# Last addition of a decoded weight piece moved from GpSimd to VectorE, and both y^T evictions put on ScalarE

## The chip, the core and the metric

The kernel runs on one core of a Trainium2 chip. The metric is device time in microseconds (us), the median of several runs. A core has five engines that work through queues of their own and wait for each other by semaphores: TensorE (PE in the profile; its weight loads are PEld), VectorE (DVE), ScalarE (ACT), GpSimd (POOL) and SyncE (SP), which here issues all DMAs. Each queue is worked in order: an instruction that waits holds up all that stand behind it on its engine.

## What is computed

The weights w_in, w_out, w1, w2, w3 and w_out2 come as float64, all else as float32. Three blocks follow each other:

```python
p_packed = sm_attn(p, k, v)             # 8 batches x 8 heads, 32 packed rows, 576 keys, head size 64
out = sm_attn(q, p_packed, p_packed)    # 576 queries against the 32 packed rows
x = out.transpose(0, 2, 1, 3).reshape(4608, 512)
h = x @ w_in                            # 512 -> 1024
solu = h * softmax(h)
y = layernorm(solu) * g_ln @ w_out      # 1024 -> 512
h2 = maximum(maximum(y @ w1, y @ w2), y @ w3)   # 512 -> 768
result = h2 @ w_out2                    # 768 -> 512
```

## The kernel before

Matrix products are done on float32 values split into a high and a low part, three products for one, so that every product of a pair of 128-row blocks stands three times in a row on TensorE.

The program has three stages. In **stage one** (to about 505 us of the span) 36 tiles of 128 tokens pass through attention (class `Packed`, two batches ahead), `tok_hidden` (the product with `w_in`, line 511, and the softmax and layer norm arithmetic around it, lines 517 to 536), `y_transpose` (four transposes into PSUM, line 577, then `lh` on ScalarE, line 583, and `ll` on VectorE, line 584) and `y_product` (line 602). `y_product` makes y^T for 512 tokens at a time in two halves of two PSUM banks, y0 and y1, with eight steps a half; each step does three products into y0 and then three into y1. When the eighth step of a half is done, both banks are copied to SBUF tiles `yt` (two buffers) by the helper `ev`, and stored to `ydram` (line 610). There are 9 blocks of 512 tokens, so 18 halves and 36 copies. The key `yt` of the table `CFG` names the engine of each: 'sv' means ScalarE for y0 (line 242) and VectorE for y1 (line 244).

Beside this, stage one **decodes weights**. A float64 weight is two 32-bit words, which are turned into float32 with arithmetic on the words. A piece of 128x256 weights (`decode_piece`) takes a load into `raw` (two buffers, line 222), one ScalarE step into `dt` (line 116), four VectorE steps (lines 121, 124, 127 and 129) and one last addition of two SBUF operands, `wt` <- `raw`, line 132. `dt` and `wt` have one buffer each. There are 56 such pieces. The first 8 belong to `w_out` (`decode_w_out2`): their `wt` is rounded into `woh` on ScalarE (line 211) and the rest into `wol` on GpSimd (line 212), and `wt` is free when both have read it. The other 48 (`decode_w2`, for w1, w2, w3 and w_out2) are stored to DRAM by a DMA (line 234), and `wt` is free when that store has landed. The key `d2` names the engine of line 132 for these pieces: 'g' is GpSimd. The larger decodes of `w_in` and of the first half of `w_out` have keys of their own (`d0`, `d1`), which stay.

The **transition** (about 505 to 560 us) ends the last block of y, reads the decoded w1 to w3 and y^T back, and splits them into parts (`split_w`, lines 650 to 657; `splits_y`, lines 724 and 725); the Newton steps that make the layer norm scales (lines 545 to 568, on 128x36 values) also start here. **Stage two** (to the end) runs 54 cells (`cell`, products on line 748, with VectorE additions `u`, `v`, `r`, `cur`, `kept` at lines 767 to 796) and the last product (line 995).

The order of instructions on each engine is not the order of the source: a list scheduler lays out all queues from its own idea of what each instruction takes. So a change of one instruction's engine also shifts others.

Of the kernel before, what the change touches and what calls it, by code (L numbers as in the profile page):

```python
# [18 lines left out]
def f32(ap):  # L19
# [7 lines left out]
    e1T='s',  # L27
    ppT='sv',
    pTz='s',
    yt='sv',  # L30
    look=3,
    s0=['LFLTFLDH', 'FFTFHD', 'FTH', 'LDFFFTDFDDHFDL'],
    s1='DFNTAHTDTyATyDyTAFy',
# [11 lines left out]
    yt_tag='e1T',  # L45
    d0='gggg',
    d1='g',
    d2='g',
    ln4='vsvs',
)  # L50

# [1043 lines left out]
```

## Time and profile before

| | us |
|---|---|
| runs before | 1118.19, 1113.46, 1114.99 |
| median | 1114.99 |
| profiled execution, device time | 1115.81 |
| its span (first to last instruction) | 1114.0 |
| PE busy | 1045.9 (94%) |
| PEld busy | 875.5 (79%) |
| VectorE busy | 734.1 (66%) |
| ScalarE busy | 480.3 (43%) |
| GpSimd busy | 274.0 (25%) |
| mean granted TensorE clock | 0.983 of full |

The span is what the trace covers; 1.8 us of the device time lie around it. Matmuls overlap, so PE that is busy throughout need not be at its peak. The shares are means over stages that differ. The rows on which the prediction rests stand in a section of their own, below.

### The profile page before, as it was taken

How to read it: one execution, taken by the hardware profiler on the slowest of the kernel's cores; microseconds unless marked ns; L12 is line 12 of the kernel's file. 1: busy time of each engine (PE TensorE's matmuls, PEld its weight loads, DVE VectorE, ACT ScalarE, POOL GpSimd, SP SyncE). 2: the span in 40 equal slices, each digit the busy share in tenths (PEclk: the TensorE clock that was granted, in tenths of full speed). 3: DMA queues.
4: the chain of work that ended last, by engine and by line, in shares of the span. 5: the costliest groups of instructions: out<-in, count | busy, mean ns of one | idle time of the engine just before them, and what ended most of it. 6: DMA issues, size and time to landing. Idle time of an engine off the chain costs nothing.

```text
span 1114.0 us, 18016 instructions
## 1 busy us (share of the span) xinstructions
PE 1045.9 (94%) x6548; PEld 875.5 (79%) x6548; DVE 734.1 (66%) x1454; ACT 480.3 (43%) x935; POOL 274.0 (25%) x283
## 2 busy tenths in 40 slices
PE   4688999999999999999789999999999999999998
PEld 2456667676767667787678999989989999998996
DVE  5778797869787886756687735735664583571560
ACT  4586766666666667456333311331131131132112
POOL 3541311111102110104576410320041041132002
PEclk9798999999999999999899999999999999999999
DMA  9752546554555623400664534534454463343421
GB/s 259 171 131 69 162 113 177 136 145 134 144 156 134 165 85 99 133 20 28 238 222 145 170 118 126 164 114 134 140 161 133 122 185 110 114 124 109 128 76 57
DMA packets 132264, 149.04 MB, mean 134 GB/s; under 512 B 51536, under 2 KB 85328, under 8 KB 132176
## 3 DMA queue, kind: packets, MB, share of 16 engines
q1 hardware_dynamic: 132176, 147.89, 45.8%
q8 instruction: 52, 0.85, 0.3%
q14 instruction: 36, 0.29, 0.1%
HBM read 113.25 MB, written 34.60 MB: 133 GB/s over the span
## 4 chain that ended last, share of the span: by engine, by line
PE 51%; DVE 6%; issue 3%; ACT 2%; POOL 2%; DMA 1%; SPq 0%; DVEq 0%; POOLq 0%; ACTq 0%
PE m L748 30%; PE o L995 13%; PE y L602 4%; PE h L511 2%; POOL s L651 1%; PE tp L577 1%; DVE s L657 1%; DMA wt<-wdram 1%; ACT u L536 0%; DVE v L787 0%; POOL al L651 0%; DVE nm L517 0%; DVE u L521 0%; DVE r L770 0%; DVE ll L584 0%
## 5 line engine op out<-in xcount | busy, mean ns | idle before, releaser
L602 PE MATMUL y<-lh,woh 128*128 128x512 f32 x288 | 118.7, 416 | 1.0 <-ACT lh L583 0.8
L783 DVE TENSOR_TENSOR u<-m,q 128x384 f32<-128x384 f32 x54 | 29.9, 553 | 133.6 <-ACT ob L1004 75.8
L602 PE MATMUL y<-ll,woh 128*128 128x512 f32 x288 | 115.9, 402 | 0.1
L602 PE MATMUL y<-lh,wol 128*128 128x512 f32 x288 | 114.7, 398 | 0.0
L779 ACT COPY q<-m 128x384 f32<-128x384 f32 x54 | 25.9, 480 | 168.4 <-PE m L748 168.2
L810 POOL TENSOR_TENSOR hl<-cur,hh 128x384 fp32r<-128x384 f32 x36 | 37.4, 1040 | 244.2 <-ACT hh L809 244.1
L132 POOL TENSOR_TENSOR wt<-raw 128x256 f32<-128x256 f32 x56 | 35.2, 628 | 244.5 <-DVE raw L129 144.3
L995 PE MATMUL o<-w2h,hh 128*128 128x512 f32 x216 | 85.3, 395 | 0.0
L995 PE MATMUL o<-w2h,hl 128*128 128x512 f32 x216 | 85.3, 395 | 0.0
L995 PE MATMUL o<-w2l,hh 128*128 128x512 f32 x216 | 85.3, 395 | 0.0
L748 PE MATMUL m<-b22h,s 128*128 128x384 f32 x216 | 65.7, 345 | 2.3 <-DVE r L770 2.0
L602 PEld LDWEIGHTS y<-lh,woh 128*128 128x128 f32 x288 | 54.0, 189 | 15.4 <-issue 2.0
L748 PE MATMUL m<-t2h,s 128*128 128x384 f32 x216 | 64.2, 337 | 0.0
L602 PEld LDWEIGHTS y<-ll,woh 128*128 128x128 f32 x288 | 55.0, 191 | 11.7 <-DVE ll L584 0.5
L602 PEld LDWEIGHTS y<-lh,wol 128*128 128x128 f32 x288 | 54.5, 189 | 12.2
L748 PE MATMUL m<-t1h,s 128*128 128x384 f32 x216 | 63.7, 335 | 0.1
L748 PE MATMUL m<-t3h,s 128*128 128x384 f32 x216 | 63.5, 334 | 0.0
L809 ACT CAST hh<-cur 128x384 fp32r<-128x384 f32 x36 | 18.5, 514 | 89.7 <-DVE cur L796 49.1
L583 ACT ACTIVATE lh<-tp,g_sb 128x512 fp32r<-128x512 f32 x72 | 47.3, 692 | 22.7 <-PE tp L577 22.4
L810 POOL TENSOR_TENSOR hl<-kept,hh 128x384 fp32r<-128x384 f32 x36 | 38.9, 1082 | 72.3 <-ACT hh L809 72.3
L771 DVE TENSOR_TENSOR kept<-r,kept 128x384 f32<-128x384 f32 x72 | 55.2, 767 | 2.0
L584 DVE SCALAR_TENSOR_TENSOR ll<-tp,g_sb,lh 128x512 fp32r<-128x512 f32 x72 | 51.8, 742 | 6.3 <-ACT lh L583 6.2
(189 smaller groups left out, 2872.1 us busy)
## 6 DMA issues: line engine op xcount, KB each, us to landing
s<-sdram SPq DMA_DIRECT2D x180, 256.0 KB, 2.9
kt<-in_k_dram SPq DMA_DIRECT2D x16, 576.0 KB, 5.2
vt<-in_v_dram SPq DMA_DIRECT2D x16, 576.0 KB, 4.8
ydram<-yt SPq DMA_DIRECT2D x36, 256.0 KB, 2.5
raw<-in_moe_w_dram SPq DMA_DIRECT2D x36, 256.0 KB, 2.8
b<-ydram SPq DMA_DIRECT2D x24, 384.0 KB, 3.4
sdram<-s SPq DMA_DIRECT2D x36, 256.0 KB, 2.1
out_dram<-ob SPq DMA_DIRECT2D x36, 256.0 KB, 2.1
```

What stands on the lines that cost most here:

```text
L132: add.tensor_tensor(out=dst, in0=f32(hi), in1=f32(lo), op=ALU.add)
L511: nc.tensor.matmul(h[:, n, :], lhsT=x, rhs=m[:, g, n * 512:(n + 1) * 512], start=(i == 0), stop=(i == len(ops) - 1),)
L583: last[nc.scalar] = nc.scalar.activation(lh, tp, AF.Copy, scale=gc)
L584: last[nc.vector] = nc.vector.scalar_tensor_tensor(out=ll, in0=tp, scalar=gc, in1=f32(lh), op0=ALU.mult, op1=ALU.subtract)
L602: nc.tensor.matmul(ys[half][m], lhsT=w[:, kc, ms], rhs=x, start=(kc == 0 and i == 0), stop=(kc == KFF - 1 and i == 2),)
L748: nc.tensor.matmul(out, lhsT=w, rhs=y, start=start and i == 0, stop=i == len(ops) - 1, skip_group_check=not start,)
L771: add(out=cur[m, n], in0=r, in1=cur[m, n], op=ALU.max)
L779: nc.scalar.copy(q, ba)
L783: add(out=u, in0=bb, in1=q, op=ALU.add)
L809: nc.scalar.copy(hh, t)
L810: nc.gpsimd.tensor_tensor(out=hl, in0=t, in1=f32(hh), op=ALU.subtract)
L995: nc.tensor.matmul(ops[i], lhsT=x[:, ts], rhs=w, start=(c == 0 and n == 0), stop=(c == KF2 - 1 and n == 2),)
```

## The change

Two keys of the table change. The last addition of the 56 decoded pieces of 128x256 goes from GpSimd to VectorE, and the copy of y1 goes from VectorE to ScalarE, so that ScalarE makes both copies of a half. No tile, buffer or DMA is added or taken away.

```diff
-    yt='sv',
+    yt='s',
...
-    d2='g',
+    d2='v',
```

How the queues move is shown at three places. In all rows a name before the arrow is the tile written and those behind it are read; the bracket names the engines or DMA queues that the instruction waits for.

The VectorE queue at a `w_out` piece, in stage one at about 110 us. Before:

```order
L535 TENSOR_TENSOR nmu<-nmu,powers 128x1 [waits DVE_49]
L121 TENSOR_SCALAR dt<-dt 128x256 [waits Activation_49]
L124 SCALAR_TENSOR_TENSOR raw<-raw,dt 128x256 [waits DMAHW6_49,DVE_49,Pool_49]
L127 TENSOR_SCALAR dt<-raw 128x256 [waits DVE_49]
L129 SCALAR_TENSOR_TENSOR raw<-raw,dt 128x256 [waits DVE_49]
L517 TENSOR_REDUCE nm<-h 128x1 [waits PE_49]
L584 SCALAR_TENSOR_TENSOR ll<-tp,g_sb,lh 128x512 [waits Activation_49] x2
```

The same place after:

```order
L535 TENSOR_TENSOR nmu<-nmu,powers 128x1 [waits DVE_49]
L121 TENSOR_SCALAR dt<-dt 128x256 [waits Activation_49]
L124 SCALAR_TENSOR_TENSOR raw<-raw,dt 128x256 [waits DMAHW6_49,DVE_49]
L127 TENSOR_SCALAR dt<-raw 128x256 [waits DVE_49]
L129 SCALAR_TENSOR_TENSOR raw<-raw,dt 128x256 [waits DVE_49]
L132 TENSOR_TENSOR wt<-raw 128x256 [waits DVE_49,Pool_49]
L517 TENSOR_REDUCE nm<-h 128x1 [waits PE_49]
L584 SCALAR_TENSOR_TENSOR ll<-tp,g_sb,lh 128x512 [waits Activation_49] x2
```

The addition of line 132 stands behind line 129 and waits there for GpSimd, which reads the piece before it out of `wt`; for the 48 later pieces it waits for the store DMA instead.

The ScalarE queue in the transition (s, ah and ch are parts of w1 to w3; the numbered y are the banks of the last two halves), as a difference:

```order
 L242 COPY yt<-y_6009 128x512
 L650 CAST s_6198<-s_6176 128x256
+L242 COPY yt<-y_6010 128x512
+L650 CAST s_6216<-s_6208 128x256
 L650 CAST ah_2_6407<-wt_6302 128x512
-L650 CAST s_6216<-s_6208 128x256
 L650 CAST s_6228<-s_6220 128x256
 L650 CAST s_6234<-s_6206 128x256
 L650 CAST s_6248<-s_6232 128x256
 L650 CAST ch_2_6465<-wt_6304 128x256
-L242 COPY yt<-y 128x512
+L242 COPY yt<-y 128x512 x2
```

The copies of y1 have joined those of y0, one a place or two behind it, and one rounding of a weight part has moved ahead of another.

The VectorE queue at the first cell of stage two (z and w are the values of the Newton steps, u and v the cell's sums, s_6441 a weight part), as a difference:

```order
 L561 TENSOR_SCALAR w<-w 128x36
+L562 TENSOR_TENSOR z<-z,w 128x36
+L559 TENSOR_TENSOR w<-z 128x36
+L560 TENSOR_TENSOR w<-w,vv 128x36
 L783 TENSOR_TENSOR u<-m_6310,q 128x384
+L561 TENSOR_SCALAR w<-w 128x36
 L562 TENSOR_TENSOR z<-z,w 128x36
+L559 TENSOR_TENSOR w<-z 128x36
 L657 TENSOR_TENSOR s_6441<-wt_6302,s_6413 128x256
 L787 TENSOR_TENSOR v<-m_6311,u 128x384
-L559 TENSOR_TENSOR w<-z 128x36
```

Five small steps have moved ahead of `v`, and the last copy `yt`, which stood five rows ahead of `u`, has gone from this queue.

## Rows read from the trace of the kernel before

**Rows 1.** Stretches: length; busy PE, PEld, DVE, ACT, POOL (instructions); clock, DMA, GB/s

```profile
100.00:505.00 405.00, 391.42 (x2895) 289.25 (x2894) 316.59 (x776) 258.97 (x509) 61.23 (x87) 1.00 0.46 126
505.00:560.00 55.00, 46.00 (x211) 38.71 (x210) 38.22 (x65) 27.23 (x53) 31.73 (x31) 0.91 0.43 146
640.00:1114.00 474.00, 467.18 (x2470) 438.26 (x2468) 244.30 (x375) 104.34 (x184) 95.04 (x76) 1.00 0.41 124
```

**Rows 2.** Chain that ended last, 376 to 505 us, share by engine and line

```profile
by line: PE y L602 25.2%; PE h L511 17.7%; PE tp L577 5.1%; ACT u L536 3.9%; DVE nm L517 3.6%; DVE u L521 3.6%; ACT h L524 3.0%; DVE Ml L248 2.4%; DVE ll L584 2.0%; DMA raw<-in_moe_w_dram 2.0%; issue 1.9%; DVE x L456 1.7%; DVE x L450 1.7%; 
```

**Rows 3.** Waits of PE (releaser: us, times, longest), 100 to 505 us; then yt's

```profile
PE tp L394 <- DVE ppz L390: 2.6, 4, 1.2
...
PEld y L602 <- DVE yt L244: 0.6, 1, 0.6
PEld y L602 <- ACT yt L242: 0.5, 1, 0.5
```

**Rows 4.** Groups of instructions: count, busy us, mean ns; third: ns min/median/max

```profile
L244 DVE COPY yt<-y 128x512 f32<-128x512 f32 x15 | 10.3, 686 | 5.5 <-PE y L602 5.3
L242 ACT COPY yt<-y 128x512 f32<-128x512 f32 x18 | 10.5, 585 | 0.0
L657 DVE TENSOR_TENSOR s<-wt,wt x9: 407/419/1511, 524.7 to 605.1; 128x256 f32<-128x256 f32 x9
```

**Rows 5.** Order of time, VectorE and GpSimd: line 129 and the addition behind it

```profile
105.39 0.43 DVE L129 SCALAR_TENSOR_TENSOR raw<-raw,dt 128x256 f32<-128x256 uint32 x1
105.95 0.61 POOL L132 TENSOR_TENSOR wt<-raw 128x256 f32<-128x256 f32 x1 [4.18 <-issue]
...
177.09 0.42 DVE L129 SCALAR_TENSOR_TENSOR raw<-raw,dt 128x256 f32<-128x256 uint32 x1
177.43 0.68 DVE L244 COPY yt<-y 128x512 f32<-128x512 f32 x1
179.85 0.61 POOL L132 TENSOR_TENSOR wt<-raw 128x256 f32<-128x256 f32 x1 [4.16 <-DMA wdram<-wt]
180.77 0.29 DVE L121 TENSOR_SCALAR dt<-dt 128x256 int32<-128x256 int32 x1 [2.66 <-ACT dt L116]
...
362.86 0.61 POOL L132 TENSOR_TENSOR wt<-raw 128x256 f32<-128x256 f32 x1 [2.80 <-DMA wdram<-wt]
...
433.25 0.43 DVE L129 SCALAR_TENSOR_TENSOR raw<-raw,dt 128x256 f32<-128x256 uint32 x1
433.81 0.61 POOL L132 TENSOR_TENSOR wt<-raw 128x256 f32<-128x256 f32 x1 [2.20 <-DVE raw L129]
```

**Rows 6.** VectorE steps beside GpSimd additions; then line 535's ns min/median/max

```profile
110.08 0.48 DVE L535 TENSOR_TENSOR nmu<-nmu,powers 128x1 f32<-128x1 f32 x1
...
412.75 0.67 DVE L360 TENSOR_SCALAR rim<-par,ri 128x2 f32<-128x2 f32 x1
...
L535 DVE TENSOR_TENSOR nmu<-nmu,powers x36: 148/160/1220, 67.1 to 508.4; 128x1 f32<-128x1 f32 x36
```

**Rows 7.** Order of time, all engines: two `w_out` pieces, the second waiting for `wt`

```profile
109.93 0.61 POOL L132 TENSOR_TENSOR wt<-raw 128x256 f32<-128x256 f32 x1 [2.12 <-issue]
...
111.65 0.43 DVE L129 SCALAR_TENSOR_TENSOR raw<-raw,dt 128x256 f32<-128x256 uint32 x1
...
112.27 0.73 POOL L212 TENSOR_TENSOR wol<-wt,woh 128x256 fp32r<-128x256 f32 x1 [1.73 <-ACT woh L211]
113.08 0.61 POOL L132 TENSOR_TENSOR wt<-raw 128x256 f32<-128x256 f32 x1
```

**Rows 8.** Order of time at the first cell: VectorE and PE

```profile
543.54 0.73 DVE L554 TENSOR_SCALAR z<-z 128x36 int32<-128x36 int32 x1
...
548.94 0.54 DVE L787 TENSOR_TENSOR v<-m,u 128x384 f32<-128x384 f32 x1
549.40 0.18 DVE L559 TENSOR_TENSOR w<-z 128x36 f32<-128x36 f32 x1
...
549.53 0.69 PE L748 MATMUL m<-t4h,ch 128*128 128x384 f32 x1 [5.08 <-DVE v L787]
```

## The prediction

> **What bounds the kernel now.** I read three views, from coarse to fine. First the busy time by stretch, to see which engine leaves no room where [rows 1]. In stage two PE is busy 467.2 of 474.0 us and VectorE 244.3, so nothing off PE counts there. In stage one (100 to 505 us) PE is busy 391.4 of 405.0 us, so 13.6 us are idle; VectorE is busy 316.6 and idle 88.4, ScalarE is busy 259.0, and GpSimd, which the change relieves, only 61.2. In the transition PE has 46.0 of 55.0 us. PE bounds stage one, but not alone: matmuls overlap, so a busy PE can still be held up a little at each step. The second view, the chain that ended last, says how often another engine holds it [rows 2]: PE's three large lines have 48.0% of the stretch from 376 to 505 us, VectorE's named lines 3.6 + 3.6 + 2.4 + 2.0 + 1.7 + 1.7 = 15.0%, ScalarE's 3.9 + 3.0 = 6.9%. Earlier the chain isn't traced; I take its shares for all of stage one. The third view, the waits, shows how little is at stake in single places: PE's largest is 2.6 us in four times, for line 390, and both copies `yt` together cost its loads 1.1 us [rows 3]. So stage two is out of reach, stage one turns a change in VectorE's load into time at about 15%, and the transition has to be read step by step.
>
> **The additions.** 56 instructions of about 0.61 us leave GpSimd [rows 5]. It is idle most of the time, so this by itself is worth nothing. 56 reach VectorE. The trace has no line 132 on VectorE; the nearest row is line 657, the same 128x256 addition of two SBUF operands there, with a median of 419 ns and up to 1511 ns where GpSimd works beside it [rows 4]. The lower bound is the step from one start to the next, 177.09 to 177.43, or 0.34 us for line 129 of the same shape [rows 5]. I take 0.42, since GpSimd will be quieter: 56 x 0.42 = 23.5 us, bounds 19.0 and, with a GpSimd step of 0.61 us in the way of one in four, 32.
>
> **The copies.** In stage one 15 copies leave VectorE, 10.3 us, and 15 x 0.585 = 8.8 us reach ScalarE [rows 4]. The other three lie in the transition. ScalarE has 146.0 us idle in stage one [rows 1]. The second copy now starts behind the first, but y0 is finished three products before y1, so ScalarE can have done the first when y1 is ready; if it hasn't, y1 comes free 0.585 us later.
>
> **Relief.** VectorE steps run longer beside a GpSimd addition: line 535, normally 0.16, takes 0.48 at 110.08, and line 360 takes 0.67 at 412.75; the longest of line 535 is 1.22 [rows 6]. Going through the order of time I find 17 such steps beside line 132, these two the first and the last, and 3.9 us above the medians of their lines. That goes. What falls beside GpSimd's other steps stays. The Trainium skill (SBUF — State Buffer, Who interferes with whom) says that a VectorE instruction with two SBUF inputs and a GpSimd instruction that reads SBUF shut each other out for a whole instruction. The 1.22 us of line 535 agrees with it; but 17 of the 56 additions met a victim, and mostly for part of their length.
>
> **The wait of the addition.** `wt` has one buffer. On GpSimd nobody stood behind an addition that waited for it; on VectorE the row reductions and the `ll` of the next products do, and behind those ScalarE and PE. How often? In 48 of the 56 pieces the addition started 0.13 us after line 129 ended (105.39 + 0.43 to 105.95 is the first of them, 433.25 + 0.43 to 433.81 the last), so it waited for nothing but the semaphore. The other eight waited 7.4 us beyond that: the first at 113.08, 1.00 us after line 129 (111.65 + 0.43), because the `w_out` piece before was still being read by line 212 until 113.00 [rows 7]; the longest at 179.85, 2.34 us, for the store; the last at 362.86 [rows 5]. At 179.85 the cover is plain: after its copy VectorE sat idle for 2.66 us until 180.77 anyway. So I charge 2 of the 7.4 us; if the cover is gone, all 7.4.
>
> **Sum for stage one.** VectorE: 23.5 - 10.3 - 3.9 + 2 = +11.3 us of load. At 15% that is +1.7 us. Bounds: 0, if its idle 88.4 us take all; and 32 - 10.3 - 3.9 + 7.4 = 25.2 us at twice the share, +7.6. ScalarE: 8.8 us at 6.9%, +0.6 us; bounds 0 and, with every second copy late, 8.8.
>
> **The transition.** PE waits 5.08 us for `v` of the first cell, which VectorE reaches through the Newton steps [rows 8]. Each of these takes 0.65 to 0.75 us while GpSimd works (0.73 at 543.54) and 0.18 afterwards (549.40). Five of them now stand ahead of `v` in addition, and the last copy, 0.68 us as at 177.43, is gone. Unhindered 5 x 0.18 - 0.68 = +0.2 us, hindered 5 x 0.73 - 0.68 = +3.0. GpSimd's work there is a fixed queue that ends at about 548.7, just ahead of `v`, so most of the five fall behind it; I take +0.4. Elsewhere in the transition the other copies that leave VectorE, 0.7 us each, stand in front of work that waits for GpSimd or for a load, so I price them at nothing; were they on the path, -1.4.
>
> **The reordering.** The scheduler's shifts in stage one have no price in any row. A transposition or a product that lands behind another wait gains or loses one PE wait, and these sum to 13.6 us of idle. Half of it either way, +-6.8 us, is my bound, and 0 the value.
>
> **Result.** +1.7 + 0.6 + 0.4 = +2.7 us. The profiled execution took 1115.8 us (span 1114.0 and 1.8 around it), 0.8 above the median of 1115.0; it would become 1118.5, and the median **1117.7 us**.
>
> **Rivals.**
>
> *The addition's wait holds VectorE up* (a wait in place of the removed copies). The in-order queue carries each of the eight waits on to `nm` or `ll`, lines that stand in the chain [rows 2]: all 7.4 us reach the end instead of 0.3. For it: the wait comes where the queue is full, and the eight pieces of `w_out` follow each other within 30 us. Against it: the 2.66 us of idle at the worst one. Price: 2.7 - 0.3 + 7.4 = +9.8, so 1124.8 us. It decides from about 3 us of the 7.4 on, when the loss passes 0.5%.
>
> *Relief outweighs.* The additions fall into VectorE's idle time and cost nothing, while the 10.3 us of copies and the 3.9 us of slowed steps lay where others waited. With the chain's non-PE share, 52%, that is -7.4 us, with +0.6 and +0.4 it is -6.4, 1108.6 us. For it: line 535 feeds line 536, 3.9% of the chain [rows 2]. Against it: PE lost only 1.1 us at `yt` [rows 3]. By the rule of the Trainium skill (SBUF — State Buffer) alone, a full shut-out by each of the 56 additions, VectorE would be freed of 56 x 0.61 = 34.2 us, 30.3 more than the trace bears out, and at 15% the end would come 4.5 us before the forecast, at 1113.2 us; I give this no chance beyond that of the rival.
>
> *It is hidden.* VectorE's 88.4 us of idle and ScalarE's 146.0 take everything in stage one, and the transition is bound by GpSimd as before: 1115.0 us.
>
> That the change doesn't do what it says is excluded: the queues after show 56 additions on VectorE and both copies of each half on ScalarE.
>
> **How the numbers follow.** Chances: forecast 0.40, hidden 0.20, held-up 0.22, relief 0.18. A measurement of this kernel can tell about 0.5% from no change, 5.6 us, so the borders are 1109.4 and 1120.6. The forecast with its reordering gives 0.36 within and 0.04 slower; hidden 0.20 within; held-up 0.19 slower, 0.03 within; relief 0.14 faster, 0.04 within. So 0.14 faster, 0.63 the same, 0.23 slower. The range leaves out the outer part of both outer cases: 1109 to 1126.
>
> **What would show it.** In the profile after: GpSimd busy about 34 us less; line 132 on VectorE at 0.42 us; the medians of line 535 unchanged but fewer long ones; ScalarE's `yt` group with 36 copies; VectorE busy about 7 us more over the span (23.5 - 12.3 - 3.9). If held up: waits of VectorE's line 132 for stores and for line 212, and PE waits for `nm` and `ll` that have grown. If relief: PE's idle in stage one well below 13.6 us. The first cell's wait for `v` should be 5 to 6 us. I am wrong if stage one ends more than 6 us off, with the clock as before, or if the first cell's wait passes 8 us.

## The result, and the profile after

| kernel | median of its runs (us) | ratio to before (95% interval) |
|---|---|---|
| before | 1114.95 | |
| after | 1121.66 | 1.0063 (1.0041 to 1.0084) |
| after, a second session (before 1114.91) | 1121.13 | 1.0056 (1.0043 to 1.0070) |

The change makes the kernel slower by 6 to 7 us. That is inside the range of the forecast and above its value: +2.7 us was forecast. The profiled execution took 1120.75 us, its span is 1119.0, 5.0 more than before; it lies 0.9 below the median of its kernel and the profiled one of before 0.9 above its own, so the two traces show 5.0 us of the 6 to 7. Below, a ratio is turned into us by ratio less 1, times 1115. Every trace is one execution, and runs of one kernel differ by 3 to 8.5 us (those of e7 below lie between 1114.7 and 1123.2), so a trace is read here for where time goes, and the ratios for how much.

The page's line of busy time after; per engine busy us, share and instructions:

```profile
PE 1046.1 (93%) x6548; PEld 877.6 (78%) x6548; DVE 741.4 (66%) x1492; ACT 488.5 (44%) x953; POOL 239.2 (21%) x227
```

GpSimd has 34.8 us less, ScalarE 8.2 and VectorE 7.3 more than the table of before shows. By stretch, after (the columns of [rows 1]):

```profile
100.00:505.00 405.00, 387.51 (x2865) 286.56 (x2865) 321.89 (x812) 263.29 (x521) 26.62 (x31) 1.00 0.45 126
505.00:560.00 55.00, 45.62 (x210) 37.67 (x210) 36.80 (x62) 28.38 (x53) 28.65 (x26) 0.94 0.38 129
640.00:1114.00 474.00, 472.11 (x2495) 442.89 (x2493) 248.00 (x378) 106.83 (x189) 97.03 (x78) 1.00 0.41 125
```

PE's idle time in stage one went from 13.6 us [rows 1] to 17.5 at the same clock. Stage two is PE-bound as before; its 4.9 us more of busy PE is only that its cells begin later and reach further into this window, which ends where the kernel before does. The start of stage two says the same. First its first product before, then after, and the first cell after (start, us, instruction, wait; [rows 8] has the cell before):

```profile
537.60 0.34 PE L748 MATMUL m<-b11h,ah 128*128 128x384 f32 x1
```

```profile
542.17 0.34 PE L748 MATMUL m<-b11h,ah 128*128 128x384 f32 x1
...
554.75 0.55 DVE L787 TENSOR_TENSOR v<-m,u 128x384 f32<-128x384 f32 x1
...
555.36 0.69 PE L748 MATMUL m<-t4h,ch 128*128 128x384 f32 x1 [6.91 <-DVE v L787]
```

Of the 5.0 us, 4.6 are there when stage two begins. The starts of line 602 show that they gather slowly: level with before at 155 us, 3.3 us behind at 210, 4.2 at 314, 6.2 at 450. A second trace of this kernel (e9 below) is 2.9 us longer than before and loses in the same way: 2.7 us ahead at 155 and 4.3 behind at 450. No single event makes the loss.

The waits of PE in stage one (releaser: us, times, longest), first before, of lines that [rows 3] leaves out, then after. Lines 330, 339, 368 and 577 are transposes and products of attention and of y. Line 394, the largest of [rows 3], hardly moved; others grew, each in one or a few places:

```profile
PE tp L577 <- DVE x L445: 1.7, 1, 1.7
...
PE tp L577 <- DVE Ml L248: 1.0, 2, 0.8
PE tp L368 <- ACT e L352: 1.0, 3, 0.5
```

```profile
PE tp L368 <- ACT e L352: 3.6, 2, 2.4
PE tp L577 <- DVE Ml L248: 2.9, 4, 1.6
PE tp L394 <- DVE ppz L390: 2.2, 5, 1.1
PE tp L330 <- ACT pT L242: 1.7, 3, 1.0
PE s L339 <- ACT kT L242: 1.7, 2, 0.9
```

The moved instructions themselves, after: the additions on VectorE (ns min/median/max) and what they waited for, then the copies, all on ScalarE:

```profile
L132 DVE TENSOR_TENSOR wt<-raw x56: 353/421/1370, 105.6 to 440.8; 128x256 f32<-128x256 f32 x56
...
  DMA wdram<-wt: 4.4, 2
  POOL wol L212: 1.4, 2
```

```profile
L242 ACT COPY yt<-y x36: 562/587/617, 122.9 to 545.3; 128x512 f32<-128x512 f32 x36
```

### The profile page after: what moved, and what is told of

The parts are those of the page before. It is cut to its first block, busy times and chain, and to the rows that moved or that the text cites. A ratio compares the mean times of both kernels' runs of the same rounds, so it can differ in the third digit from the quotient of the medians.

```text
span 1119.0 us, 17956 instructions
## 1 busy us (share of the span) xinstructions
PE 1046.1 (93%) x6548; PEld 877.6 (78%) x6548; DVE 741.4 (66%) x1492; ACT 488.5 (44%) x953; POOL 239.2 (21%) x227
## 4 chain that ended last, share of the span: by engine, by line
PE 44%; DVE 3%; issue 3%; POOL 2%; ACT 1%; DMA 1%; SPq 0%; DVEq 0%; POOLq 0%; ACTq 0%
PE m L748 31%; PE o L995 13%; POOL s L651 1%; DVE s L657 1%; DMA wt<-wdram 1%; DVE v L787 0%; POOL al L651 0%; DVE u L783 0%; DVE r L770 0%; ACT lh L583 0%; POOL hl L810 0%; DVE w L559 0%; DVE b21l L725 0%; ACT s L650 0%; DVE t3l L725 0%
## 5 line engine op out<-in xcount | busy, mean ns | idle before, releaser
L472 POOL TENSOR_TENSOR allarge<-y,ahlarge 128x640 fp32r<-128x640 f32 x8 | 12.4, 1552 | 201.5 <-ACT ahlarge L471 201.5
L519 ACT ACTIVATE u<-h,nm 128x1024 f32<-128x1024 f32 x36 | 40.2, 1116 | 32.8 <-DVE nm L517 32.7
```

The costliest lines, as they stand in the source:

```text
L472: (nc.vector if CFG['al'] == 'v' else nc.gpsimd).tensor_tensor(out=al, in0=y, in1=f32(ah), op=ALU.subtract)
L519: nc.scalar.activation(u, hv, AF.Exp, bias=nm, accum_out=sums[:, t:t + 1])
```

## Experiments

Three theories ran against each other. **W**: VectorE's queue waits in the addition for the one buffer of `wt`. **L**: the added load of VectorE, or of ScalarE by the copies (**S**), makes it. **O** (R in the first texts): the scheduler's new order of all queues makes it, whatever engine the moved steps run on. Each block shares one session's runs of before, unless said otherwise.

### One part alone, a control, and a second buffer

```diff
 e1_add_on_vector        +    d2='v',
 e2_copies_on_scalar     +    yt='s',
 e3_copies_swapped       +    yt='vs',     (y0 on VectorE, y1 on ScalarE)
 e4_no_wait_for_wt       both keys of the change, and in decode_piece:
-        t = dec_p.tile([P, DC], F32, tag="dt", name="dt", bufs=1)
-        wt = dec_p.tile([P, DC], F32, tag="wt", name="wt", bufs=1)
-        return wt, *decode(wt, raw, t, add=ENG[CFG['d2']])
+        wt = dec_p.tile([P, DC], F32, tag="wt", name="wt", bufs=2)
+        return wt, *decode(wt, raw, wt, add=ENG[CFG['d2']])
```

> Only the last addition of the 56 pieces goes to VectorE; y1 is still copied by VectorE. Theory L (VectorE's load and the addition's wait cost stage one its time): 23.5 us of load without the 10 us that the copies take away, so more than the whole change, +7 to +10 us over before. Theory R (the shifted order of the queues decides, not the load): anywhere within +-6 us. Theory S (both copies on ScalarE cost the time): about 0 to +2 us.

> Only y1's copy goes to ScalarE; the additions stay on GpSimd. Theory L: VectorE loses 10 us of load in stage one, so -1 to -3 us against before. Theory R: anywhere within +-6 us. Theory S: +4 to +6 us, nearly the whole loss.

> A control: the kernel before with y0 copied by VectorE and y1 by ScalarE, so that no engine has more or less to do and only the order of the queues shifts. Theories L and S: within +-1.5 us of before. Theory R: a move of 3 us or more either way, which would then be the size of what order alone does.

> The whole change, but the addition writes into the tile that ScalarE's step filled (two buffers, no separate wt tile, the same memory), so that line 132 on VectorE never waits for the store or for GpSimd. In the profile after these waits are 4.4 + 1.4 = 5.8 us. Theory L with the wait as its larger part: 3 to 6 us faster than the changed kernel, 1116 to 1118. Theory L with the load as its larger part: 0 to 2 us faster, 1120 to 1122. Theory R: anywhere from 1115 to 1127.

| run | median (us) | ratio (95%) | us by ratio |
|---|---|---|---|
| before | 1113.97 | | |
| e1_add_on_vector | 1117.04 | 1.0025 (1.0012 to 1.0037) | +2.8 |
| e2_copies_on_scalar | 1116.16 | 1.0020 (1.0010 to 1.0030) | +2.2 |
| e3_copies_swapped | 1118.58 | 1.0047 (1.0030 to 1.0064) | +5.2 |
| e4_no_wait_for_wt | 1113.14 | 0.9990 (0.9975 to 1.0006) | -1.1 |

The control is the surprise: it only swaps the copies of y0 and y1 between the engines, and it loses 5.2 us, against 2.8 and 2.2 for the two parts of the change. The additions alone cost less than L expected, and the copies less than S expected, where L expected a gain. And the change with two buffers costs nothing: 7 to 8 us less than the change, though line 132's waits above are only 5.8 us. Its 1113.14 us lie below what any theory expected. W would not give back more than there was, and e4 has another order too, so the order had to be taken apart from the rest.

### The order held fixed

The instructions that the program emits are the same one by one in all these kernels; only engines, buffers and the order on the queues differ. So the order of one kernel can be forced on another: at the end of the program each instruction gets an ordering edge (no semaphore) to the one that should stand before it on its engine. A moved instruction stands where it stood in the other program's overall sequence. The edges add no instruction: the kernel before with its own order forced on it builds to the same program. No such pinned copy was timed. In the order of after, 421 of 5780 matmuls and 349 of the 1400 VectorE instructions that both have stand at another place than in that of before.

```diff
     with _tile.TileContext(nc) as tc:
         tile_packed_attention_solu_ln_maxout_kernel(tc, *args)
+        pin(tc)
...
+def pin(tc):
...
+    for step in steps:
+        at += step
+        i = traced.get(f"I-{at}")
...
+        before = last.get(i.engine)
+        if before is not None:
+            tc.add_manual_dep(
+                i, before, mybir.DependencyInfo(mybir.DependencyClass.NoSync, mybir.DependencyReason.DATA), reason="order"
+            )
+        last[i.engine] = i.name
```

> The whole change (56 additions on VectorE, both copies on ScalarE), but every queue is pinned to the order of the kernel before: each engine works its instructions in the sequence in which they stood there, and the moved ones stand where they stood in the whole program's sequence. Before is taken as 1114.0 in the same session, after as about 1120.7 (ratio 1.0063). Theory O (the loss comes from the shifted order of all queues): 1113 to 1116. Theory W (the loss comes from VectorE waiting in the addition for the one buffer of wt): the wait stays, 1118 to 1122. Theory L (VectorE's added load alone): 1118 to 1122, with the visible waits of the addition unimportant.

> The engines of the kernel before (additions on GpSimd, second copy on VectorE), but every queue is pinned to the order of the changed kernel. Theory O: it takes over the loss, 1118 to 1122. Theories W and L: the load and the wait are those of before, 1112 to 1116. If both order and load count by half each: about 1117.

> The changed kernel in exactly its own order on every queue, with the decode steps working in place in a tile of two buffers, so that the addition need not wait for the store or for line 212. Theory W: the loss goes, 1113 to 1116. Theories O and L: it stays, 1118 to 1122, since order and load are the same. The earlier run with two buffers (1113.1) had another order too, so this run says which of the two edits gave its 8 us.

> The change with two buffers as in the run before, in the order of the kernel before. Theory W: equal to the run before within 1.5 us, 1113 to 1116. Theory O: equal to the change in the order of before, 1113 to 1116, and 4 to 7 us below the run with two buffers in the order of after. Theory L: 1117 to 1121 here too.

> The changed kernel once more, with more runs, in one session with the next three. Theory W+O (the loss is the sum of a wait of about 2 us and of an order that fits worse): 1120 to 1122, at least 1.5 us above the 1119.1 of the same order with two buffers. Theory O alone: 1118 to 1120, no more than with two buffers.

> Only the second copy of each half goes to ScalarE, and every queue is pinned to the order of before. With the scheduler's own order this edit took 2.2 us. Theory O: those came from the order, so 1113.5 to 1115. Theory S (the copies themselves delay ScalarE's other steps): 1116 to 1118, and then the copies are a good half of the 4.4 us that the whole change costs in the order of before.

> The kernel before (additions on GpSimd, second copy on VectorE) with the tile of two buffers and the order that the scheduler makes for it. If two buffers help by themselves: 1108 to 1111, and the 1113.1 of the change with two buffers would still hold a loss of 3 us. If they only take away the wait that the change made: 1113 to 1116. If any new order costs some us: 1116 to 1119.

> The kernel before with two buffers, each queue pinned to the order that the scheduler made for the change with two buffers (the run that took 1113.1). Theory O (that order is good whatever the engines): 1111 to 1114. Theory M (an order is good only with the engines it was made for; before in the order of after took 1118.6): 1116 to 1119.

In the table "engines" says where the additions and second copies run, "buffers" whether `wt` has one or two, "order" whose order the queues have. Before was 1114.4 for e5 to e8, 1114.91 for e9 to e12, and 1113.97 for e4, which is repeated from above.

| run | engines | buffers | order of | median (us) | ratio (95%) | us by ratio |
|---|---|---|---|---|---|---|
| e10 | copies moved | 1 | before | 1115.25 | 1.0010 (0.9998 to 1.0023) | +1.1 |
| e8 | after | 2 | before | 1118.07 | 1.0028 (1.0017 to 1.0039) | +3.1 |
| e5 | after | 1 | before | 1118.77 | 1.0039 (1.0025 to 1.0052) | +4.3 |
| e6 | before | 1 | after | 1118.63 | 1.0039 (1.0025 to 1.0053) | +4.3 |
| e7 | after | 2 | after | 1119.08 | 1.0039 (1.0023 to 1.0056) | +4.3 |
| e9 | after | 1 | after | 1121.13 | 1.0056 (1.0043 to 1.0070) | +6.2 |
| e12 | before | 2 | e4 | 1116.08 | 1.0011 (0.9999 to 1.0023) | +1.2 |
| e4 | after | 2 | e4 | 1113.14 | 0.9990 (0.9975 to 1.0006) | -1.1 |
| e11 | before | 2 | e11 | 1125.14 | 1.0098 (1.0081 to 1.0115) | +10.9 |

**The order alone moves the time by up to 9 us.** e11 and e12 are the same instructions on the same engines with the same buffers in one session, 1125.14 and 1116.08 us; e7 and e4 are such a pair too, 4.3 against -1.1 in two sessions, and their intervals do not touch. No expectation had e11's loss; the highest was 1119. Stage one by stretch, e11 and then e12, and the PE waits that differ most (releaser: us, times, longest):

```profile
100.00:505.00 405.00, 383.00 (x2844) 284.02 (x2843) 313.32 (x765) 254.68 (x501) 61.60 (x87) 0.99 0.45 126
```

```profile
PE tp L393 <- DVE ppz L389: 6.0, 6, 2.7
PE tp L329 <- ACT pT L241: 4.5, 6, 1.1
PE tp L576 <- DVE powers L527: 3.5, 1, 3.5
```

```profile
100.00:505.00 405.00, 389.74 (x2881) 290.69 (x2880) 313.37 (x774) 258.49 (x507) 61.55 (x87) 1.00 0.46 126
```

```profile
PE tp L394 <- DVE ppz L390: 1.8, 5, 0.8
PE tp L330 <- ACT pT L242: 1.7, 2, 1.4
```

(Lines count one less in e11.) VectorE is busy 313.3 and 313.4 us in the two: the load is equal. PE is idle 22.0 and 15.3 us. The three waits make 14.0 us in e11, the first two 3.5 in e12, where the third is not listed. Where in the queues the decisive swaps lie was not taken further apart.

**The order of after costs the engines of before 4.3 us** (e6), which W and L had put at nothing. But **the engines of after cost 4.3 us in the order of before** too (e5), which O had put at nothing. Together they make 6 to 7, less than the plain sum of 8.6, though the intervals don't exclude that sum. Of the 4.3 in e5, the copies are 1.1 (e10, whose interval reaches zero), and what is left with two buffers is 3.1 (e8). W alone is out: e7, in the order of after and without the wait, still loses 4.3 us where W expected none. e5's additions still wait, e8's don't (ns min/median/max and releasers; e5, then e8, where the list of releasers is empty):

```profile
L132 DVE TENSOR_TENSOR wt<-raw x56: 382/424/1316, 102.6 to 436.2; 128x256 f32<-128x256 f32 x56
...
  DMA wdram<-wt: 3.1, 3
  POOL wol L212: 1.0, 1
```

```profile
L132 DVE TENSOR_TENSOR wt<-raw x56: 382/424/1309, 105.6 to 438.7; 128x256 f32<-128x256 f32 x56
its engine sat idle before it (us, times) until:
who waited for it (us, times):
```

So 4.1 us of waits are worth about 1.2 in that order, and in that of after 5.8 are worth about 1.9 (e9 less e7). Both differences are smaller than the intervals: a wait that matters by 1 to 2 us is what the runs suggest, and none at all is not excluded. The second buffer shows no gain by itself: before with it took 10.9 and 1.2 us more in the two orders in which it ran, the second with an interval that reaches zero.

PE's waits tell order and engines apart in part, because traces of one order repeat them. First e6, the engines of before in the order of after; then e8, the engines of after in the order of before:

```profile
PE tp L577 <- DVE Ml L248: 3.1, 4, 1.7
...
PE tp L368 <- ACT e L352: 0.9, 2, 0.6
```

```profile
PE tp L577 <- DVE x L445: 2.9, 1, 2.9
```

Line 577's wait for `Ml`, 2.9 us after, is as long in e6, and 0.8 to 1.0 in the four traces with the order of before: it comes with the order. Line 368's wait for `e` is 3.6 us after, 3.5 and 3.2 in e9 and e7 with the same order and engines, and 0.9 in e6: it needs both. And in the order of before, line 577's one wait for `x` grows from 1.7 us, also 1.7 in e10, to 3.0 and 2.9 in e5 and e8, which have the additions on VectorE.

**An order fits engines.** In the order of e4 the engines of after lose nothing (e4), while in the two other orders they lose 3 to 7 us. That it suits the engines of after better than those of before (e12, at the lower edge of the 1116 to 1119 that this theory expected) is not shown, since these two intervals overlap. No kernel here is faster than before beyond its interval; e4 comes nearest, with -1.1 us (-2.8 to +0.7).

## Why the prediction was off in size

The time is inside the range, but the range was 17 us wide, and on the prediction's own chances a loss of more than 0.5% had only 0.23. The sign came out right; the term that the sum had put at nothing, the new order, turned out about as large as the others together.

**The additions: right in duration.** 421 ns median against the 0.42 taken from line 657 [rows 4], and VectorE's busy time rose by 7.3 us where about 7 was forecast. But that sum agrees by two errors that cancel: too much for the additions, and a relief that did not come. Where the next step follows at once, an addition takes only 0.34 us from its start to the next one's, the lower bound of the forecast, which would be 19.0 us for 56 (after, in order of time):

```profile
109.35 0.42 DVE L132 TENSOR_TENSOR wt<-raw 128x256 f32<-128x256 f32 x1
109.69 0.15 DVE L532 TENSOR_SCALAR powers<-powers 128x1 int32<-128x1 int32 x1
```

**Relief: this term failed.** 3.9 us of slowed VectorE steps were to go with line 132, worth 0.6 us at 15%. They went, and others came. Going through the order of time from 100 to 510 us, I add what VectorE steps beside a GpSimd step take beyond the median of their line and shape: 8.7 us before, of which 3.9 beside line 132 and 2.8 beside line 472 (GpSimd's subtraction for the attention values); 8.9 after, of which 7.9 beside line 472, in eight hits. One of them: the same step of line 472 before (GpSimd, then VectorE beside it) and after.

```profile
336.77 1.55 POOL L472 TENSOR_TENSOR allarge<-y,ahlarge 128x640 fp32r<-128x640 f32 x1 [10.90 <-ACT ahlarge L471]
```

```profile
336.98 0.77 DVE L445 STREAM_TRANSPOSE x<-st 128x256 f32<-128x256 f32 x2
337.68 0.10 DVE L523 TENSOR_SCALAR nmu<-su 128x1 f32<-128x1 f32 x1
337.71 0.73 DVE L584 SCALAR_TENSOR_TENSOR ll<-tp,g_sb,lh 128x512 fp32r<-128x512 f32 x1
```

```profile
343.25 1.56 POOL L472 TENSOR_TENSOR allarge<-y,ahlarge 128x640 fp32r<-128x640 f32 x1 [52.51 <-ACT ahlarge L471]
```

```profile
342.37 0.74 DVE L584 SCALAR_TENSOR_TENSOR ll<-tp,g_sb,lh 128x512 fp32r<-128x512 f32 x1
343.02 0.77 DVE L445 STREAM_TRANSPOSE x<-st 128x256 f32<-128x256 f32 x2
343.71 1.37 DVE L132 TENSOR_TENSOR wt<-raw 128x256 f32<-128x256 f32 x1
```

Before, the two transpositions and the product of a PSUM tile stood there, at their usual 0.39 and 0.73 us. After, the product stands ahead of the transpositions, and the moved addition behind them meets line 472 and takes 1.37 us. The trace agrees in this with the rule of the Trainium skill that the prediction named (SBUF — State Buffer, Who interferes with whom): an instruction of VectorE with two SBUF inputs contends with a GpSimd instruction that reads SBUF, and one with at most one SBUF input, outside the modes that use both ports, does not. But steps with one SBUF input were hit too. Four of the eight hits are lines 121 and 127, which read one SBUF tensor each; here line 127, of 0.29 us by its median (whether it ran in such a mode, the trace doesn't tell):

```profile
148.65 1.20 DVE L127 TENSOR_SCALAR dt<-raw 128x256 int32<-128x256 int32 x1
```

That the order decides what is hit, the pinned runs show: beside line 472 the excess is 2.8 to 3.0 us in the four kernels with the order of before (before, e5, e8, e10) and 5.3 to 8.6 in all others but e2 (2.8). In e5 and e8 the relief came as forecast: the whole excess fell from 8.7 to 4.5 us. It still left them slower than before, and e4 has 6.6 beside line 472 and is no slower than before, so this is one thing that the order moves, and not what decides the time.

**The load as a whole: right within its bounds.** The additions and copies without the wait, in the order of before, are e8: +3.1 us (1.9 to 4.3). The forecast for these was 1.7 less 0.3 for the wait, plus 0.6, so +2.0. So VectorE's 15% of the chain [rows 2] as a weight is not contradicted in the sum. In its parts it fits less well: the copies alone were to gain 0.9 us (10.3 us less at 15%, and 0.6 more for ScalarE), and taking them off VectorE gained nothing (e10, +1.1, from -0.2 to 2.6).

**The addition's wait: a smaller price than the rival's, a larger one than the sum's.** 5.8 us in four waits were seen, 7.4 in eight were feared. The three longest after (each with steps behind it on VectorE):

```profile
112.51 0.43 DVE L132 TENSOR_TENSOR wt<-raw 128x256 f32<-128x256 f32 x1 [1.02 <-POOL wol L212]
113.95 1.22 DVE L517 TENSOR_REDUCE nm<-h 128x1 f32<-128x1024 f32 x1 [1.02 <-PE h L511]
```

```profile
181.26 0.43 DVE L132 TENSOR_TENSOR wt<-raw 128x256 f32<-128x256 f32 x1 [2.79 <-DMA wdram<-wt]
182.01 1.22 DVE L517 TENSOR_REDUCE nm<-h 128x1 f32<-128x1024 f32 x1 [0.33 <-PE h L511]
...
293.85 0.43 DVE L132 TENSOR_TENSOR wt<-raw 128x256 f32<-128x256 f32 x1 [1.62 <-DMA wdram<-wt]
...
294.52 1.21 DVE L517 TENSOR_REDUCE nm<-h 128x1 f32<-128x1024 f32 x1
```

Behind the first two, line 517 still had to wait for PE's product: the cover that the prediction saw at 179.85 [rows 5] held. Behind the third it did not: line 517 follows without a wait of its own. PE then waits 0.81 us at 300.46 for `kT` from ScalarE; e9 has such a wait too, of 0.88, and e7, the same order without the wait of line 132, has none. That the one makes the other was not traced step by step. Charged were 0.3 us, suggested are 1 to 2. The rival, with all 7.4 on the path, is not what happened, though its time of 1124.8 is as close to the result as the forecast, 3 to 4 us each.

**The transition: right in the sum, wrong in its step.** +0.4 was forecast; 4.6 us of loss at the first product of stage two and 5.0 at the end make +0.4, and in e9 2.7 and 2.9. But the first cell waited 6.91 us for `v`, 1.8 more than before, where 5 to 6 were forecast. Three of the five Newton steps that moved ahead of `v` came behind GpSimd's work and took 0.17 to 0.20 us; the other two ran beside it:

```profile
551.49 1.27 POOL L632 TENSOR_TENSOR w2l<-wt,w2h 128x512 fp32r<-128x512 f32 x1
552.71 0.73 POOL L651 TENSOR_TENSOR s<-s,s 128x256 fp32r<-128x256 f32 x1
```

```profile
551.62 1.19 DVE L559 TENSOR_TENSOR w<-z 128x36 f32<-128x36 f32 x1
552.84 0.65 DVE L560 TENSOR_TENSOR w<-w,vv 128x36 f32<-128x36 f32 x1
```

The end agrees because other waits of PE were shorter: from 505 to 600 us it waited 9.3 us for `v` in four times before, and 8.9 in two after. The forecast had no such term, so that its sum came out is luck.

**The reordering: this value failed.** It was put at 0 with a bound of 6.8 us to either side, "half of the idle time". With the engines of before, the order of after costs +4.3 us (e6); with the second buffer e11's and e12's come with +10.9 and +1.2, and the control, with its two copies swapped, took +5.2. None of these gained beyond its interval, and one went past the bound. The value 0 took order for noise about a middle. A row that speaks against it, as an argument and not as a thing that the runs show, is PE's 13.6 us of idle in stage one [rows 1]: with so little idle there is little to gain by another order, while no row bounds what it can lose. With the +4.3 of e6, known only now, the same sum would come out at 1119 to 1122, the lower end if part of it is the load's loss counted twice.

## What to carry to other kernels

Where a scheduler lays out the queues, an edit is two edits: the work that it moves, and the new order. The second was no noise around zero here: with 13.6 us of idle PE in stage one, no order gained beyond its interval and one lost 10.9. Before blaming or praising the first, run the new engines in the old order and the old engines in the new order; the sum of the moved instruction's own waits did not tell them apart here. And work taken from GpSimd need not free VectorE: look at what then stands beside GpSimd's other steps.

## What was not expected of the hardware

A 128x256 addition on VectorE, 0.42 us by its record, holds its queue for only 0.34 us when the next step follows at once (109.35 to 109.69); the forecast had that as a bound and not as its value. And GpSimd's steps of line 472, 1.29 and 1.55 us long, 12 or 13 of its 16 between 100 and 510 us, go with 2.8 to 8.6 us of longer VectorE steps there, as which instruction stands beside them changes with the order.
